# A fused attention and feed-forward layer on one core: nine fills, the first tile's path, the burst form and the instruction order changed together

## The chip, the cores and the metric

The kernel runs on one core of one Trainium2 chip. A core has five engines with instruction streams of their own: TensorE (PE in the profile; its weight loads are PEld), VectorE (DVE), ScalarE (ACT), GpSimd (POOL) and SyncE (SP), which issues most DMAs. The metric is the device time in microseconds; three runs of the kernel before gave 149.11, 149.41 and 149.48, so the median is 149.41.

## The reference

```
xn = layernorm(x)                                   # x: 1 x 2048 x 448, no scale or shift
q, k, v = split(xn @ wqkv)                          # 16 heads of 28
s = softmax(q . k[t - 2j], j = 0..7) @ v[t - 2j]    # 8 taps, dilation 2, masked before the start
s = s @ wo                                          # 448 x 448
h = gelu(xn @ w1 + b1)                              # 448 x 1792
g = silu(h @ w2 + b2)                               # 1792 x 448
out = x + s * g
```

Inputs and output are bf16.

## The kernel before

The 2048 positions are taken as two halves (even and odd positions, so that dilation 2 becomes neighbours) and cut into 16 tiles of 128; four tiles make a chunk (`c` 0 to 3). The work per tile or chunk:

- `stats`, `rstds`, `norm` (lines 432 to 517): layer norm statistics on DVE, the inverse root by ACT (square root) and DVE (reciprocal) for tiles 0 to 3 and by POOL for the others, scaling on DVE, a copy of the last 64 columns (POOL or DVE, line 482), then xn transposed: by TensorE with copies out of PSUM for tiles 0 to 3, by a transposing DMA on SP's queue for the others.
- `qk_rows` and `vproj`: q, k and v from xn; `ff1` and `ff2`: the two layers of the feed-forward part; `final`: the product with `wo`, then product with g and addition of x (`gated`).
- `attn`: nine visits of 228 positions. The scores (line 809, four PSUM banks), exponentials on ACT (line 818), masks on DVE (line 824), then P V (line 843, a burst of 64 small matmuls on eight 64x32 tiles of the array), whose result DVE transposes (line 855), normalises (859, 863) and transposes back (880).

448 rows are three and a half k-tiles. So two products of the same size run as a pair on the upper and lower half of the array (`pair`): first four passes, then a nop on POOL or SP that tells the second half it may start (line 574), then three passes with the halves exchanged. The first two tiles run as full-array matmuls instead (`first_batch`), three k-tiles for each of q, k, v, and the half k-tile at the end.

The eight PSUM banks are shared by all products. Two passes of a neighbouring pair are laid inside most P V bursts (`INSIDE`); the burst's sequence is a string in which a digit stands for one P V matmul on a tile of the array and a letter for one strip of the laid-in pass. `BURSTS` gives each visit its string: EVEN for visits 0, 3 and 4, LATER for 1, 6 and 8, MIXED[0] for 2 and 5, MIXED[1] for 7.

The order is written out. The code first adds every step as a task with engine, cost, dependencies and pool slots; `ORDER` then lists task numbers (a negative number n means task -n - 1 on its second engine), and instructions are issued in that order on each engine, so each engine runs its own sub-sequence strictly in order. The costs and `rate` and `tail` numbers of the tasks serve only to choose buffers and to leave out fill matmuls whose planned start is after 8.0 us (line 339). Those fills (lines 336 to 340, nine of 512 columns, then of 128) keep TensorE running until the first real product.

DMA loads (lines 363 to 427): tile 0's x goes out on ACT's queue, tile 1's on SP's; of `w_in` k-tile 1 on ACT, the rest on SP; the bias b1 (`b1r`, transposed by TensorE at line 1043 and copied at 1045) on POOL's. `w1` comes in two halves of three DMAs each on SP (line 982).

Of the kernel before, what the change touches and what calls it, by code (L numbers as in the profile page):

```python
# [28 lines left out]
ORDER = [  # L29
# [42 lines left out]
]  # L72
LAST = 352
TWICE = (5, 6, 7, 8, 9, 10)
QUEUE = 20
HOPS = ("POOL", "POOL")
MASK_ON = ("DVE", 0.4)


def VISITS(bs):  # L80
    out = []
# [119 lines left out]
def kernel(  # L201
# [12 lines left out]
    nc = tc.nc  # L214
# [187 lines left out]
    def ktiles(ap):  # L402
        return ap.rearrange("(k p) c -> p k c", p=P)


    load_x(0, 1, "ACT", tail=1.65)
    load_x(1, 1, "SP", tail=1.2)
    t_w = []

# [725 lines left out]
```

## Time and profile before

| | |
|---|---|
| median of three runs | 149.41 us |
| the profiled execution | 148.85 us, of which the span from first to last instruction 147.1 us |
| ACT busy, largest group | 102.1 us; 56 GELU activations of 128x512, 687 ns each |
| DVE busy, largest group | 108.4 us; 18 transpositions of 128x512 f32, 700 ns each |
| PE, instructions on the chain that ended last | 92% of the span |
| granted TensorE clock | 0.999 |
| DMA | 19.49 MB, 132 GB/s over the span |

The profile comes from one execution. Lines are those of the kernel's file; the helpers' lines stand for many callers: 526 is every matmul of the dense products, 325 and 323 are copies out of PSUM by DVE and by ACT, 330 is every fill, 365 and 388 DMA issues. In the views an entry is followed, in brackets, by the idle time of its engine before it and by what released it. The time that TensorE is busy is modelled from the issue of its pipelined matmuls.

### The profile page before, as it was taken

The page shows a single profiled execution, that of the slowest core. Times are in us where ns is not written, and L with a number is a line of the kernel's source. Part 1 is how long each engine was busy: PE and PEld are TensorE (multiplying, and loading weights), DVE is VectorE, ACT ScalarE, POOL GpSimd, SP SyncE. Part 2 cuts the span into 40 slices and gives each one's busy share as a digit, 9 for nine tenths or more (in the row PEclk, how much of TensorE's full clock was granted, in tenths as well). Part 3 has the DMA queues.
Part 4 walks back from the last instruction along what each step waited for, and adds up shares of the span by engine and source line. Part 5 has one row for each costly group of instructions (what it writes and reads, how often), then busy time and mean ns, then how long its engine had stood idle before and what let it go on. Part 6 is the DMA issues. An engine that isn't in the chain of part 4 may idle for free.

```text
span 147.1 us, 5485 instructions
## 1 busy us (share of the span) xinstructions
PE 142.4 (97%) x2273; PEld 76.1 (52%) x2273; DVE 108.4 (74%) x272; ACT 102.1 (69%) x190; POOL 29.1 (20%) x83
## 2 busy tenths in 40 slices
PE   7899999999999999999999999999999999999991
PEld 2554444444445555556555655445485454555460
DVE  2878440099555769889796988977799979699963
ACT  3459688675659487876887796985997587965320
POOL 4113570105154031612301002040001000010001
PEclk9999999999999999999999999999999999999999
DMA  4999946999759998799983498303501001002212
GB/s 107 385 328 322 134 107 137 269 159 271 185 104 159 151 242 130 174 137 207 147 193 92 138 126 166 107 21 86 170 6 36 4 0 36 4 0 62 62 67 65
DMA packets 39495, 19.49 MB, mean 132 GB/s; under 512 B 26631, under 2 KB 38762, under 8 KB 39470
## 3 DMA queue, kind: packets, MB, share of 16 engines
q1 hardware_dynamic: 38206, 17.25, 56.8%
q0 software_dynamic: 688, 1.31, 3.8%
q10 hardware_dynamic: 576, 0.57, 1.1%
q8 instruction: 18, 0.29, 0.9%
q14 instruction: 7, 0.06, 0.1%
HBM read 9.42 MB, written 3.94 MB: 91 GB/s over the span
## 4 chain that ended last, share of the span: by engine, by line
PE 92%; DMA 3%; issue 1%; DVE 1%; ACT 0%; POOL 0%; ACTq 0%; DVEq 0%; POOLq 0%
PE bank L526 82%; PE bank L764 3%; DMA E<-in_B_b_dram 3%; PE bank L809 3%; PE bank L843 3%; PE bank L942 1%; DVE sg L954 1%; ACT E L818 0%; PE bank L509 0%; DVE o L961 0%; PE bank L1043 0%; POOL E L330 0%; PE bank L762 0%; PE bank L493 0%; PE bank L338 0%
## 5 line engine op out<-in xcount | busy, mean ns | idle before, releaser
L526 PE MATMUL bank<-xnT,w 64*128 64x512 bf16 (+1 forms) x428 | 46.2, 376 | 0.0
L714 ACT ACTIVATE h<-bank,b 128x512 bf16<-128x512 f32 x56 | 35.5, 687 | 13.8 <-PE bank L526 13.5
L526 PE MATMUL bank<-w,h 64*128 64x448 bf16 (+1 forms) x440 | 41.8, 349 | 0.0
L526 PE MATMUL bank<-w_in,xnT 64*128 64x448 bf16 (+2 forms) x342 | 36.3, 350 | 0.0
L526 PEld LDWEIGHTS <-w 64*128 64x128 bf16 (+1 forms) x428 | 19.3, 93 | 21.2
L526 PEld LDWEIGHTS <-h 64*128 64x128 bf16 (+1 forms) x440 | 19.6, 93 | 14.7
L526 PEld LDWEIGHTS <-xnT 64*128 64x128 bf16 (+2 forms) x342 | 16.1, 94 | 14.5 <-issue 0.4
L818 ACT ACTIVATE E<-bank 128x456 bf16<-128x456 f32 (+1 forms) x36 | 17.1, 555 | 2.7 <-PE bank L809 2.6
L323 ACT CAST qk_tok<-bank 128x448 bf16<-128x448 f32 x26 | 13.3, 537 | 5.9 <-PE bank L526 5.4
L855 DVE STREAM_TRANSPOSE wide<-bank 128x512 f32<-128x512 f32 x18 | 12.6, 700 | 3.1 <-PE bank L843 3.1
L876 POOL COPY wide<-wide 64x64 bf16<-64x64 bf16 x20 | 5.5, 279 | 43.5 <-PE bank L526 16.2
L880 DVE STREAM_TRANSPOSE oT<-wide 128x512 bf16<-128x512 bf16 x18 | 12.0, 692 | 1.5 <-POOL wide L876 1.5
L824 DVE TENSOR_TENSOR E<-E,m_gen 128x456 bf16<-128x456 bf16 (+1 forms) x32 | 11.7, 377 | 0.9 <-ACT E L818 0.9
L526 PE MATMUL bank<-wo,oT 64*128 64x448 bf16 x98 | 11.5, 349 | 0.2 <-ACT E L818 0.2
L776 DVE TENSOR_TENSOR wide<-bank,b 128x448 f32<-128x448 f32 x15 | 9.2, 619 | 3.1 <-PE bank L526 3.0
L434 DVE BATCH_NORM_STATS2 st<-x_sb 128x6 f32<-128x448 bf16 x16 | 9.7, 609 | 2.0 <-DMA x_sb<-in_A_x_dram 2.0
L863 DVE TENSOR_TENSOR wide<-wide,rd 128x448 bf16<-128x448 f32 x18 | 11.0, 614 | 0.2
L474 DVE TENSOR_SCALAR xn<-x_sb,mv,rstd 128x448 bf16<-128x448 bf16 x16 | 6.3, 397 | 5.8 <-POOL rstd L456 5.2
L325 DVE CAST v_tok<-bank 128x448 bf16<-128x448 f32 x4 | 2.5, 615 | 9.0 <-PE bank L526 9.0
L694 ACT ACTIVATE kd<-qkT,head 128x1024 bf16<-128x1024 bf16 x8 | 8.9, 1159 | 0.0
L843 PEld LDWEIGHTS <-v 64*32 64x32 bf16 x576 | 6.9, 89 | 3.6 <-issue 3.5
L788 ACT ACTIVATE wide<-wide 128x448 f32<-128x448 f32 x12 | 6.7, 578 | 2.3 <-DVE wide L776 2.3
(78 smaller groups left out, 141.3 us busy)
## 6 DMA issues: line engine op xcount, KB each, us to landing
v<-v_hbm SPq DMA_DIRECT2D x17, 128.0 KB, 3.5
v_hbm<-v_tok SPq DMA_DIRECT2D x11, 128.0 KB, 2.9
w<-in_B_w_dram SPq DMA_DIRECT2D x2, 672.0 KB, 6.3
out_dram<-o SPq DMA_DIRECT2D x9, 112.0 KB, 1.7
x_sb<-in_A_x_dram SPq DMA_DIRECT2D x4, 224.0 KB, 2.8
w<-in_B_w_dram SPq DMA_DIRECT2D x2, 448.0 KB, 6.1
w_in<-in_A_wqkv_dram SPq DMA_DIRECT2D x2, 336.0 KB, 4.2
w<-in_B_w_dram SPq DMA_DIRECT2D x2, 336.0 KB, 5.4
```

Of the source, the lines that this page charges most:

```text
L323: nc.scalar.copy(o, i)
L434: nc.vector.bn_stats(out=buf(p_st, k)[:], in_=x_sb[:, t, :])
L526: return nc.tensor.matmul(ps[rows, :n], lhsT[:, rows], rhs, start=start, stop=stop)
L694: nc.scalar.activation(dst, src, ACT.Copy, scale=head[:, a:a + 1])
L714: nc.scalar.activation(buf(p_h, own, i)[:], buf(p_b, own, i)[:], ACT.Gelu_apprx_tanh, bias=b1[:, mt:mt + 1])
L776: nc.vector.tensor_tensor(out=buf(p_y, k)[:, :n], in0=buf(p_b, own, i)[:, :n], in1=b2[:, cs], op=ALU.add)
L818: nc.scalar.activation(buf(p_E, k)[:, :8 * n], buf(p_b, a, at + i)[:, :8 * n], ACT.Exp, scale=SCALE)
L824: nc.vector.tensor_tensor(out=E, in0=E, in1=m[:, :, :, :n].rearrange("p i g q -> p (i g) q"), op=ALU.mult)
L843: nc.tensor.matmul(banks[a][32 * g:32 * g + 32, c0:c0 + n], buf(*v_at[b])[r, s, 2 * g + h, :], buf(p_E, exps[2 * h + s // 2])[r, c1:c1 + n ...
L855: nc.vector.transpose(buf(p_dt, k)[:], buf(p_b, po, a)[:])
L863: nc.vector.tensor_tensor(out=turned_in(d[a]).rearrange("p l b c -> p (l b) c")[:, :, :DH], in0=buf(p_dt, d[a])[:].rearrange("p (b c) -> p ...
L880: nc.vector.transpose(oT[:, a::2, q:q + 256], turned_in(d[a]).rearrange("p l b c -> p l (b c)"))
```

## The change

The two added steps of tile 0 (a second part of its normalisation and of its first copy) shift the later task numbers by two, so all of `ORDER` is written anew. The diff, cut to its core:

```diff
-EVEN = TILES * 3 + STRIPS + TILES * 2 + STRIPS + TILES * 3
-LATER = TILES * 3 + STRIPS + TILES * 2 + TILES[:2] + STRIPS + TILES[2:] + TILES * 2
-MIXED = ("436501724360172435067123eadcbhfg623765334147675655acbhefd6g020101742051420751432",
-         "376124057613405271634527agfhdebc014212031050311500gedhcfab6466473642573257632475")
-BURSTS = [EVEN, LATER, MIXED[0], EVEN, EVEN, MIXED[0], LATER, MIXED[1], LATER]
+BURST_OF = TILES * 3 + STRIPS + TILES * 2 + STRIPS + TILES * 3
...
-    t_qz = [plan.add("DVE", 0.08, memset("vector", q[:, :, :, DH:], 0.0), [t_on]) for q in qk_tok]
-    t_vw = [plan.add("DVE", 0.08, memset("vector", v[:, :, :, DH:], 1.0), [t_on]) for v in v_tok]
-    t_kz = plan.add("DVE", 0.12, memset("vector", qkT[:, :, :, :PAD], 0.0), [t_on])
+    t_qz = [plan.add("POOL", 0.2, memset("gpsimd", q[:, :, :, DH:], 0.0), [t_on]) for q in qk_tok]
+    t_vw = [plan.add("POOL", 0.2, memset("gpsimd", v[:, :, :, DH:], 1.0), [t_on]) for v in v_tok]
+    t_kz = plan.add("POOL", 0.2, memset("gpsimd", qkT[:, :, :, :PAD], 0.0), [t_on])
...
-    load_x(0, 1, "ACT", tail=1.65)
-    load_x(1, 1, "SP", tail=1.2)
+    load_x(0, 1, "SP", tail=1.55)
+    load_x(1, 1, "ACT", tail=1.3, issue=0.5)
...
     def norm(t):
-        def f1(k):
-            nc.vector.tensor_scalar(buf(p_xn, k)[:, :D], x_sb[:, t, :], mv[:, t, 0:1], rstd[:, t:t + 1],
-                                    op0=ALU.subtract, op1=ALU.mult)
-        a = plan.add("DVE", 0.40, f1, [t_rs[t]], take=(p_xn,))
-
-        if not t:
-            t_st[1].deps.append(a)
+        cuts = (0, 2 * P, D) if not t else (0, D)
+        scaled = []
+        for lo, hi in zip(cuts, cuts[1:]):
+            def f1(k, lo=lo, hi=hi):
+                nc.vector.tensor_scalar(buf(p_xn, scaled[0] if scaled else k)[:, lo:hi], x_sb[:, t, lo:hi], mv[:, t, 0:1],
+                                        rstd[:, t:t + 1], op0=ALU.subtract, op1=ALU.mult)
+            scaled.append(plan.add("DVE", 0.40 if not lo and hi == D else 0.09 + (hi - lo) / 1440.0, f1, [t_rs[t]] + scaled,
+                                   take=() if scaled else (p_xn,)))
+        a = scaled[0]
...
-            def f4(k, k0=n * i, b=b):
-                copy(k.on, xnT[:, k0:k0 + n, t * P:(t + 1) * P], half_bank(buf(p_b, b))[:, k0:k0 + n, :])
...
+            for k0, k1 in ((0, 1), (1, 2)) if not t and not i else ((n * i, n * i + n),):
+                def f4(k, k0=k0, k1=k1, b=b):
+                    copy(k.on, xnT[:, k0:k1, t * P:(t + 1) * P], half_bank(buf(p_b, b))[:, k0:k1, :])
...
-            for c in BURSTS[b]:
+            for c in BURST_OF:
```

Besides these, only planned costs change (DMA rate 262 to 330 and 230 to 290, the tails, `bn_aggr` 0.18 to 0.12, b1's tail 3.2 to 4.75), and `ORDER`. Its new text, read as tasks, orders the places that matter here so:

- TensorE at the start: before, 20 fills ahead of tile 0's first two transpositions; now 11, then tile 1's first two transpositions, two fills, tile 0's first two, a fill, tile 1's other two, the first matmuls of tile 1 (q and v on k-tile 0), tile 0's other transpositions, and then matmuls of both tiles in turn. b1's transposition comes behind nine of these matmuls; before it came ahead of the first. Behind it, tile 3's transpositions now stand ahead of the pair qk(2), which they followed before.
- DVE at the start: the zero fill of `zero` (line 1018), eps, half, statistics and aggregate of tile 1, the same of tile 0, reciprocal and `norm` of tile 1, reciprocal of tile 0, `norm` of tile 0 in two parts (columns 0 to 255, 256 to 447), the copy of its k-tile 0, statistics and aggregate of tile 2, the copy of its k-tile 1. Before: eight fills, eps and half among them, statistics and aggregate of tile 0, statistics of tile 1, reciprocal and `norm` of tile 0, aggregate of tile 1, copy of tile 0's first two k-tiles.
- ACT: square roots of tile 1, then 0, then the copies of tile 1's two halves out of PSUM.
- POOL: the fill and DMA of b1, four of the nine fills with the identity between them, the copies of tiles 1 and 0 (line 482), a fill, tile 2's copy, a fill, tile 3's copy; two `v_tok` fills stand ahead of the nops of v(2) and ff1(0, 0), the fill of `qkT` ahead of that of ff1(0, 6). The two mask tiles (line 1032) and `head` (line 359) come later than before.
- SP: as before up to the second half of `w1`; then the padding store of `v_hbm` (line 1019, earlier than before), the first transposing DMA of q and k (tile 0), and only then the last of the three pieces of `w1`.
- Pairs up to wo(0): some change places, v(4) and qk(4), ff2(0) and ff2(4), qk(9) and qk(10), qk(11) and the v pairs around it, v(12) and qk(13) to qk(15). From wo(0) on the pairs, scores and bursts stand in the old order but for swaps inside ff1 chunk 3.
- DVE between the bursts of visits 6 and 7: before, the order was sum of ff2's tile 8 with b2 (line 776), gate of tile 6 (792), product of tile 6 (956), sum of tile 9 (776), a mask, the first transposition of burst 6 (855). Now: gate of tile 6, sum of tile 8, a mask, the first transposition of burst 6, its reciprocal, product of tile 6, addition of x for tile 6, the second transposition of burst 6, gate of tile 8, masks and other steps, the sums of tiles 11 and 10, a reciprocal, the sum of tile 9.

More of the change, by code (lines that the diff above doesn't have):

```diff
@@ L393, with load_x @@
     t_x = {}
-    def load_x(t0, n, eng="SP", deps=(), tail=1.6):
+    def load_x(t0, n, eng="SP", deps=(), tail=1.6, issue=0.45):
         src = rows(x_half, t0 * P, n * P).rearrange("(t p) d -> p t d", p=P)
         d = dma(eng, x_sb[:, t0:t0 + n, :], src, 112 * n, deps,
-                rate=262.0 if t0 < 2 * TPC else 230.0, tail=tail, share=n if eng == "SP" else 0)
+                issue=issue, rate=330.0 if t0 < 2 * TPC else 290.0, tail=tail, share=n if eng == "SP" else 0)
         for t in range(t0, t0 + n):
@@ L403, in ktiles @@
         return ap.rearrange("(k p) c -> p k c", p=P)
-    load_x(0, 1, "ACT", tail=1.65)
-    load_x(1, 1, "SP", tail=1.2)
+    load_x(0, 1, "SP", tail=1.55)
+    load_x(1, 1, "ACT", tail=1.3, issue=0.5)
     t_w = []
     def load_w(kt, tail, eng="SP"):
-        t_w.append([dma(eng, w_in[:, kt, :], A_wqkv[kt * P:(kt + 1) * P, :], 336, rate=262.0, tail=tail, share=1)])
-    load_w(0, 1.8)
-    load_w(1, 1.2, "ACT")
-    load_x(2, 1, "SP", tail=1.5)
-    load_w(2, 1.55)
-    load_x(3, 1, "SP", tail=1.6)
+        t_w.append([dma(eng, w_in[:, kt, :], A_wqkv[kt * P:(kt + 1) * P, :], 336, rate=330.0, tail=tail, share=1)])
+    load_w(0, 2.2)
+    load_w(1, 1.6, "ACT")
+    load_x(2, 1, "SP", tail=2.3)
+    load_w(2, 1.75)
+    load_x(3, 1, "SP", tail=1.95)
     tails = A_wqkv[KF:D, :].rearrange("p (w d) -> p w d", d=D)
-    t_w.append([dma("SP", w_in3[:64], tails[:, 0:3:2, :], 112, issue=0.6, rate=262.0, tail=1.7),
-                dma("SP", w_in3[64:], tails[:, 1:3, :], 112, issue=0.6, rate=262.0, tail=1.7)])
+    t_w.append([dma("SP", w_in3[:64], tails[:, 0:3:2, :], 112, issue=0.6, rate=330.0, tail=2.0),
+                dma("SP", w_in3[64:], tails[:, 1:3, :], 112, issue=0.6, rate=330.0, tail=2.0)])
     t_b1z = plan.add("POOL", 0.1, memset("gpsimd", b1r, 0.0), [t_on])
     t_b1r = dma("POOL", b1r[:NMT], B_b1.rearrange("(m f) -> m f", f=P), 4, [t_b1z])
-    t_b1r.tail = 3.2
+    t_b1r.tail = 4.75
     t_root = plan.add("ACT", 0.2, lambda _: nc.scalar.activation(sd[:, NT - 1:], eps_t[:], ACT.Sqrt), [t_eps], table=("sqrt",))
@@ L434, in f1 @@
             nc.vector.bn_stats(out=buf(p_st, k)[:], in_=x_sb[:, t, :])
-        k = plan.add("DVE", 0.63, f1, t_x[t], take=(p_st,))
+        k = plan.add("DVE", 0.64, f1, t_x[t], take=(p_st,))
         def f2(_):
             nc.vector.bn_aggr(out=mv[:, t, :], in_=buf(p_st, k)[:])
-        t_st[t] = plan.add("DVE", 0.18, f2, [k], give=((p_st, k, 0),))
+        t_st[t] = plan.add("DVE", 0.12, f2, [k], give=((p_st, k, 0),))
     t_rs = {}
@@ L472, in norm @@
     def norm(t):
-        def f1(k):
-            nc.vector.tensor_scalar(buf(p_xn, k)[:, :D], x_sb[:, t, :], mv[:, t, 0:1], rstd[:, t:t + 1],
-                                    op0=ALU.subtract, op1=ALU.mult)
-        a = plan.add("DVE", 0.40, f1, [t_rs[t]], take=(p_xn,))
-        if not t:
-            t_st[1].deps.append(a)
+        cuts = (0, 2 * P, D) if not t else (0, D)
[7 more added lines that the diff above has]
+        a = scaled[0]
         def f2(k):
             (nc.gpsimd if k.on == "POOL" else nc.vector).tensor_copy(buf(p_xn, a)[:, D:], buf(p_xn, a)[:, KF:D])
-        twice = t_dup[t] = plan.add("POOL" if t < TPC else "DVE", 0.28 if t < TPC else 0.18, f2, [a])
+        twice = t_dup[t] = plan.add("POOL" if t < TPC else "DVE", 0.28 if t < TPC else 0.18, f2, scaled[-1:])
         if t >= TPC:
@@ L512, in norm @@
             halves.append(b)
-            def f4(k, k0=n * i, b=b):
-                copy(k.on, xnT[:, k0:k0 + n, t * P:(t + 1) * P], half_bank(buf(p_b, b))[:, k0:k0 + n, :])
-            t_xT[t] = plan.add(("DVE", "ACT"), (dve(n * P, 2), act(n * P)), f4, [b] + ([t_xT01[t]] if i else []), give=((p_b, b, 0),))
-            t_xT01.setdefault(t, t_xT[t])
+            for k0, k1 in ((0, 1), (1, 2)) if not t and not i else ((n * i, n * i + n),):
+                def f4(k, k0=k0, k1=k1, b=b):
+                    copy(k.on, xnT[:, k0:k1, t * P:(t + 1) * P], half_bank(buf(p_b, b))[:, k0:k1, :])
+                w = (k1 - k0) * P
+                t_xT[t] = plan.add(("DVE", "ACT"), (dve(w, 2), act(w)), f4, [b] + ([t_xT[t]] if k0 else []), give=((p_b, b, 0),) if k1 > 1 else ())
+                t_xT01.setdefault(t, []).append(t_xT[t])
     def behind(later, earlier):
@@ L614, in f1 @@
                         j.part(buf(p_b, own or k), kt, 2, kt == 0, False)
-                    f[i, q, kt] = plan.add("PE", pe(D), f1, ([t_xT01[tiles0 + i]] if kt < 2 else j.deps[:1]) + t_w[kt] + ([f[i, q, kt - 1]] if kt else []),
+                    f[i, q, kt] = plan.add("PE", pe(D), f1, (t_xT01[tiles0 + i][:1 + kt * (not i and not tiles0)] if kt < 2 else j.deps[:1]) + t_w[kt] + ([f[i, q, kt - 1]] if kt else []),
                                            take=() if kt else (p_b,))
@@ L983, in load_w1 @@
         cs = slice(i * F // 2, (i + 1) * F // 2)
-        t_w1.append([dma("SP", w1[:, 0:3, cs], ktiles(B_w1[0:KF, cs]), 672, deps, rate=262.0, tail=1.3, share=3)]
-                    + [dma("SP", w1[64 * i:64 * i + 64, 3, cs], B_w1[KF:D, cs], 112, deps, rate=262.0, tail=1.3) for i in range(2)])
+        t_w1.append([dma("SP", w1[:, 0:3, cs], ktiles(B_w1[0:KF, cs]), 672, deps, rate=330.0, tail=2.1, share=3)]
+                    + [dma("SP", w1[64 * i:64 * i + 64, 3, cs], B_w1[KF:D, cs], 112, deps, rate=330.0, tail=2.0) for i in range(2)])
     load_w1(0, [])
@@ L1056 @@
         t_w2[i // 2].append(dma("SP", w2[:, lo:hi, :], B_w2[lo * P:hi * P, :].rearrange("(m p) c -> p m c", p=P),
-                                112 * (hi - lo), first, rate=230.0, share=hi - lo))
+                                112 * (hi - lo), first, rate=290.0, share=hi - lo))
     t_b2 = dma("POOL", b2[:], B_b2.rearrange("(o d) -> o d", o=1).to_broadcast((P, D)), 112, turned)
```

84 rows, old and new, of the table ORDER are left out of this document.

## The prediction

> **What bounds the kernel now.** I read the page's totals first.
>
> ```profile
> span 147.1 us, 5485 instructions
> PE 142.4 (97%) x2273; PEld 76.1 (52%) x2273; DVE 108.4 (74%) x272; ACT 102.1 (69%) x190; POOL 29.1 (20%) x83
> ```
>
> Then busy time by stage (columns: stretch in us, its length, then busy us and instruction count of PE, PEld, DVE, ACT, POOL, then granted clock, DMA share, GB/s).
>
> ```profile
> 6.04:11.41 5.37, 5.37 (x51) 2.92 (x49) 3.92 (x14) 3.07 (x9) 0.71 (x3) 1.00 1.07 340
> 11.41:46.63 35.22, 35.22 (x358) 16.90 (x356) 18.24 (x56) 25.73 (x43) 12.30 (x33) 1.00 0.89 184
> 46.63:103.29 56.66, 56.66 (x1203) 31.25 (x1196) 47.45 (x110) 43.25 (x83) 11.44 (x28) 1.00 0.79 140
> 103.29:105.00 1.71, 1.47 (x15) 0.59 (x12) 1.62 (x4) 1.70 (x3) 0.00 (x0) 1.00 0.62 184
> 105.00:143.15 38.15, 38.15 (x627) 21.42 (x627) 32.97 (x70) 26.17 (x51) 1.95 (x9) 1.00 0.12 35
> 143.15:147.10 3.95, 0.79 (x19) 0.64 (x16) 1.40 (x4) 0.25 (x1) 0.84 (x1) 0.97 0.20 60
> ```
>
> TensorE is busy without a hole from 6.04 to 143.15, but for 1.71 - 1.47 = 0.24 us after 103.29. Busy need not mean full pace, so I check one stretch against its work further down. The start comes next, in order of time (start us, duration us, engine, line, operation, output<-input).
>
> ```profile
> 0.81 0.41 ACTq L365 DMA_DIRECT2D x_sb<-in_A_x_dram  x1
> 0.82 0.20 POOL L330 MEMSET E<- 128x128 bf16 x1 [0.29 <-POOLq L1119]
> 0.82 0.39 SPq L365 DMA_DIRECT2D x_sb<-in_A_x_dram  x1
> ...
> 0.86 4.03 PE L338 MATMUL bank<-const-bfloat16-1.0 128*128 128x512 bf16 x20 [0.86 <-PEq L1119]
> 0.90 0.11 DVE L330 MEMSET qkT<- 128x64 uint32 x1 [0.90 <-PEq L1119]
> ...
> 3.38 0.63 DVE L434 BATCH_NORM_STATS2 st<-x_sb 128x6 f32<-128x448 bf16 x1 [1.98 <-DMA x_sb<-in_A_x_dram]
> 4.04 0.18 DVE L438 BATCH_NORM_AGGREGATE mv<-st 128x2 f32<-128x6 f32 x1
> 4.14 0.60 DVE L434 BATCH_NORM_STATS2 st<-x_sb 128x6 f32<-128x448 bf16 x1
> 4.26 0.29 ACT L446 ACTIVATE sd<-mv,eps_t 128x1 f32<-128x1 f32 x1 [1.24 <-DVE mv L438]
> ...
> 4.65 0.15 DVE L449 RECIPROCAL rstd<-sd 128x1 f32<-128x1 f32 x1
> 4.83 0.40 DVE L474 TENSOR_SCALAR xn<-x_sb,mv,rstd 128x448 bf16<-128x448 bf16 x1
> ...
> 5.29 0.28 PE L509 MATMUL bank<-ident,xn 128*128 128x128 bf16 x2 [0.40 <-DVE xn L474]
> ...
> 5.61 0.29 DVE L325 COPY xnT<-bank 128x256 bf16<-128x256 bf16 x1 [0.29 <-PE bank L509]
> ...
> 6.04 0.73 PE L526 MATMUL bank<-w_in,xnT 128*128 128x448 bf16 x3
> ...
> 6.19 0.37 ACT L323 COPY xnT<-bank 128x256 bf16<-128x256 bf16 x1 [0.54 <-PE bank L509]
> ```
>
> The head is a chain of small steps on one tile: x lands (3.38), statistics, square root, reciprocal, scaling, transposition, copy, first real matmul at 6.04. The last view is the chain of waits.
>
> ```profile
> 5.81 0.23 PE bank L1043
> ...
> 6.77 0.11 PE bank L509 x2
> ...
> 7.56 1.70 PE bank L526 x9
> ...
> 54.11 0.21 PE bank L843 x24
> ...
> 55.00 5.78 PE bank L526 x60
> ...
> 90.95 0.20 PE bank L843 x24
> ...
> 91.76 9.20 PE bank L526 x86
> ...
> 100.96 0.21 PE bank L843 x20
> ...
> 101.76 1.05 PE bank L526 x10
> ...
> 126.29 0.21 PE bank L843 x24
> ...
> 127.19 9.59 PE bank L526 x100
> ```
>
> Two transpositions cost 0.11 us of TensorE (6.77). Nine 448-column matmuls take 1.70, or 0.189 each, so 512 columns take 0.216. By the order list, 74 passes of 448 columns and 98 of 512 lie between 11.41 and 46.63: 74 x 0.189 + 98 x 0.216 = 35.2 us, against a stretch of 35.22. TensorE waits for nothing there. So a change can gain only before 6.04, in the 0.24 us, in the nine P V bursts, or in the last 3.95 us; anything else can only lose. A P V burst lasts from its first L843 piece to the long piece behind it: 0.89 (visit 0) and 0.81 (visit 4) in the form EVEN, 0.80 (visit 5) in MIXED[0], 0.90 (visit 8) in LATER.
>
> **The change part by part, against the profiled execution (148.85 us, of which 147.1 are span; the runs' median of 149.41 lies 0.56 above it).**
>
> *Head.* In the new list tile 1, now loaded by ACT, goes first, with tile 0 behind it. Tile 1's x takes the queue place that tile 0's had (0.81), so I let its statistics start at 3.38 too. But tile 0's statistics and aggregate now stand on VectorE before tile 1's reciprocal: statistics 4.14, and 0.66 later (as 3.38 to 4.04) the aggregate at 4.80; the reciprocal follows 0.10 behind it (as 4.04 to 4.14), at 4.90 instead of 4.65. That is +0.25. The first copy goes to ACT: 0.37 instead of 0.29, +0.08. The first real matmul comes at 6.04 + 0.33 = 6.37. TensorE has then more behind it: before, the transpositions of tile 1 (four) came after 6.04; now these four are done, and of tile 0 the first two: against the chain of before, four fewer stand behind the start, -0.22. The transposition of b1, at 5.81 in the shade of the copy before, is now inside the stream (about 0.06, half of the 6.77 row), and one more fill matmul may be too (0.05). Net +0.33 - 0.22 + 0.11 = **+0.22**. From below, with tile 1's x 0.2 us earlier and no fill, 0; from above +0.5, because the copy of tile 0's second k-tile now stands behind tile 2's statistics (0.63) and would end only just before the matmul that reads it. Cutting tile 0's normalisation and copy in two costs VectorE some 0.15 + 0.1 us of fixed cost, hidden, since tile 1's matmuls (three at 0.19) and a transposition cover them; without that cover it would be 0.25.
>
> *Fills.* VectorE loses nine fills of 0.11 us, most of them in the 1.98 us in which it waits for x anyway: gain 0. GpSimd takes nine at about 0.20 (the row at 0.82): 1.8 us on an engine busy 20% of the span. Four stand before the first copy of xn, the rest between copies and the nops that release the second half of a row-tile pair; a nop is at most 0.2 us later, and TensorE has another product (four passes, 0.76) in between. 0; without that cover 0.2 each for the two that stand ahead of a nop.
> The Trainium skill's page "SBUF — State Buffer", section "Who interferes with whom", says that VectorE in its two-port modes and GpSimd lock each other out for a whole instruction, which speaks against this move; by it a fill beside a normalisation would add up to 0.2 us to that tile, off the path for all but the first tile.
>
> *Bursts.* Six of nine change form. With EVEN at (0.89 + 0.81)/2 = 0.85, three MIXED lose 0.05 each and three LATER gain 0.05 each: **0**. Bounds with EVEN at 0.81 or 0.89: 3 x 0.01 - 3 x 0.09 = -0.24 and 3 x 0.09 - 3 x 0.01 = +0.24.
>
> *Queues.* SP now issues the last piece of w1 behind the first transposing DMA of q and k, and the padding store moves ahead of it.
>
> ```profile
> w<-in_B_w_dram SPq DMA_DIRECT2D x4, 112.0 KB, 6.3
> ...
> 11.13 3.76 SPq L388 DMA_TRANSPOSE qkT<-qk_tok  x2
> ```
>
> One such transposition holds SP for 1.9 us, so the piece goes out near 13.0 and lands by 19.3. The pair that first reads it (ff1, chunk 0, products 6 and 7) starts 18 passes of 448 and 21 of 512 behind the point that was 11.41: 11.63 + 18 x 0.189 + 21 x 0.216 = 19.6, and reads the fourth k-tile another 3 x 0.216 = 0.65 later. Margin about 0.9: cost 0, at most +0.5.
>
> *The rest of the list.* From the wo(0) pair on, TensorE's own order is the old one but for swaps inside chunk 3 of ff1, and in the first 100 us pairs only change places: no pass is added or dropped. The 0.24 us after 103.29 stay, since scores 6, their exponentials and the wo pair keep their order; the tail's order too. 0, with -0.24 from below.
>
> **Sum:** +0.22 + 0 + 0 + 0: 149.07 for a profiled execution of 148.85, and 149.41 + 0.22 = 149.6 as a median.
>
> **The rivals.** *A hole behind visit 8's scores (slower).*
>
> ```profile
> 109.60 0.62 DVE L776 TENSOR_TENSOR wide<-bank,b 128x448 f32<-128x448 f32 x1
> ...
> 110.79 0.62 DVE L956 SCALAR_TENSOR_TENSOR sg<-bank,g 128x448 bf16<-128x448 f32 x1
> 111.33 0.61 DVE L776 TENSOR_TENSOR wide<-bank,b 128x448 f32<-128x448 f32 x1
> ...
> 112.78 0.43 PE bank L809 x32
> ```
>
> The scores at 112.78 need four of eight PSUM banks. The sum of tile 9 (111.33), which frees a bank at 111.94, stands in the new list behind the sums of tiles 11 and 10, which themselves wait for products after these scores; so its bank is lost to them. The running pair holds two; so both the product of tile 6 (110.79, now behind a 0.7 us transposition and a reciprocal, hence done near 112.4) and the banks of burst 6 decide, of which one may still be held. VectorE has about 0.4 us of margin. If it runs later than that, TensorE waits for the rest; two f32 steps and a transposition late (2 x 0.54 + 0.7 = 1.8) would cost 1.4, half of that lateness 0.5, so I price it at 0.9: 149.6 + 0.9 = 150.5. For it: VectorE is busy 32.97 of 38.15 us in that stretch. Against: the exponentials free their banks earlier.
>
> *Bursts and hole both pay (faster):* EVEN at visit 4's 0.81 everywhere (-0.24), the 0.24 us after 103.29 gone, and the head at its lower bound of 0: 149.41 - 0.48 = 148.9. For it: visits 0 and 4 differ by 0.08 in one and the same form, so the form's own price is not known better than that. Against: nothing in that wait's order changed.
>
> *TensorE slows down again (slower).* Eleven fill matmuls, not 20, now stand before the first transposition. The eleven narrow ones of the 4.03 us take about 0.055 each, so the nine wide ones took 3.43, or 0.38 each, against 0.216 for 512 columns later: it starts at half pace. After the change fills end near 4.4, and until 6.37 there are only six transpositions and a few fills; before the hole was 0.40 (5.29). If pace halves again for about 3 us, 1.5 are lost: 151.1.
> The Trainium skill's page "TensorE: Matmul & The Clock Gate", Part 1, says that the clock falls back after an idle window of about 3.4 us; by that rule the 2 us here would not do it, and no run here shows it yet.
>
> **How the numbers follow.** What a measurement of this kernel can tell from no change is about 0.3%, 0.45 us: 148.96 to 149.86. The sum's own outcome (149.6, own range 149.1 to 150.0) gets 0.45, the hole 0.26, the faster case 0.22, the slow TensorE 0.07. Over its bounds the sum's case gives 0.04 to faster, 0.33 to same, 0.08 to slower; the faster case gives 0.21 to faster and 0.01 to same; the other two are slower. That makes faster 0.25, same 0.34, slower 0.41. The range runs from 148.7 (the faster case with a head 0.2 earlier) to 150.9 (the hole at its dearer end), which leaves out the slow TensorE and the rarer ends.
>
> **What would show it.** Right: tile 1's reciprocal near 4.90, the first real matmul near 6.37, the stretch from there full, the wait after 103.3 still about 0.24, bursts of 0.80 to 0.90. Wrong: idle TensorE rows released by VectorE ahead of scores or bursts; matmuls near 0.38 us pace after 6; a wait for w1 near 20; or a head that starts before 6.04, which would mean that x landed at another time than I let it.

## The result, and the profile after

| | before | after |
|---|---|---|
| median | 149.13 us (15 runs, 148.75 to 149.48) | 150.02 us (15 runs, 149.48 to 150.49) |
| profiled execution | 148.85 us, span 147.1 | 149.49 us, span 147.5 |

The ratio is 1.0054, with a 95% interval of 1.004 to 1.0068: the change makes the kernel slower by about 0.8 us (0.89 by the two medians). Ratios leave out single executions that lie more than 1.5% above the fastest of their kernel (one each in runs 2, 8 and 12 below), while the medians of those runs count them. Both profiled executions are at the lower end of their runs; a second profile of after comes as the last experiment.

The page of after gives these totals, and the view by stage has the columns of the prediction's (stretch, length, busy us and count of PE, PEld, DVE, ACT, POOL, granted clock, DMA share, GB/s).

```profile
PE 142.0 (96%) x2263; PEld 74.2 (50%) x2263; DVE 107.7 (73%) x265; ACT 101.6 (69%) x190; POOL 31.0 (21%) x92
```

```profile
6.44:11.22 4.78, 4.78 (x42) 2.48 (x41) 3.76 (x13) 2.31 (x8) 0.93 (x5) 1.00 1.07 305
11.22:45.80 34.58, 34.58 (x351) 16.37 (x348) 17.75 (x55) 25.92 (x43) 11.79 (x30) 1.00 1.12 213
45.80:103.18 57.38, 57.38 (x1195) 31.34 (x1186) 47.16 (x109) 45.10 (x85) 12.73 (x34) 1.00 0.61 127
103.18:105.00 1.82, 1.82 (x50) 1.08 (x44) 1.78 (x5) 1.58 (x5) 0.00 (x0) 1.00 0.22 63
105.00:142.76 37.76, 37.76 (x628) 20.23 (x625) 32.92 (x70) 24.23 (x47) 2.27 (x9) 1.00 0.14 40
142.76:147.50 4.74, 0.79 (x19) 0.65 (x16) 1.39 (x4) 0.25 (x1) 0.85 (x1) 1.00 0.18 50
```

TensorE is now full in every stretch up to 142.76, also where 0.24 us were idle before (103.18 to 105.00). It ends its main work at 142.76, 0.39 us earlier than before (143.15). The last stretch is 4.74 us instead of 3.95. So a kernel whose TensorE has finished earlier ends later.

Four places differ. First the start (timeline of after; start, duration, engine, line, operation).

```profile
3.58 0.63 DVE L430 BATCH_NORM_STATS2 st<-x_sb 128x6 f32<-128x448 bf16 x1 [2.35 <-DMA x_sb<-in_A_x_dram]
...
5.07 0.13 DVE L445 RECIPROCAL rstd<-sd 128x1 f32<-128x1 f32 x1
...
5.74 0.59 DVE L473 TENSOR_SCALAR xn<-x_sb,mv,rstd 128x256 bf16<-128x256 bf16 x2
...
5.69 0.28 PE L507 MATMUL bank<-ident,xn 128*128 128x128 bf16 x2 [0.65 <-DVE xn L473]
...
6.15 0.28 PE L507 MATMUL bank<-ident,xn 128*128 128x128 bf16 x2
...
6.44 0.55 PE L526 MATMUL bank<-w_in,xnT 128*128 128x448 bf16 x2
...
6.01 0.37 ACT L319 COPY xnT<-bank 128x256 bf16<-128x256 bf16 x1 [0.53 <-PE bank L507]
```

The first real matmul is at 6.44 (before 6.04). The scores of visit 1, in the chains of waits (start, length, what) of before and of after:

```profile
51.03 0.43 PE bank L809 x32
```

```profile
51.53 0.43 PE bank L809 x32
```

They start 0.50 later.

Second, the bursts (chain of waits of after).

```profile
54.61 0.21 PE bank L843 x24
...
55.40 6.35 PE bank L526 x66
...
125.35 0.21 PE bank L843 x24
...
126.16 10.24 PE bank L526 x106
```

Visit 0 takes 0.79 (before 0.89), visit 8 takes 0.81 (before 0.90); the nine sum to 7.29 us against 7.59. The form isn't all of it: visit 1, which now has EVEN, takes 0.91 in after, 0.85 before, and 0.78 with EVEN in run 3.

Third, the wait after the scores of visit 6. This is ScalarE around it, first before, then after.

```profile
103.11 1.28 ACT L818 ACT_TABLE_LOAD   x1 [1.61 <-PE bank L809]
104.40 1.88 ACT L818 ACTIVATE E<-bank 128x456 bf16<-128x456 f32 x4
```

```profile
101.21 0.68 ACT L714 ACTIVATE h<-bank,b 128x512 bf16<-128x512 f32 x1
101.91 1.28 ACT L818 ACT_TABLE_LOAD   x1
103.43 1.88 ACT L818 ACTIVATE E<-bank 128x456 bf16<-128x456 f32 x4 [0.24 <-PE bank L809]
```

Before, ScalarE's load of the table for the exponential (1.28 us) starts only when the scores are there: the engine is idle for 1.61 us in front of it, and the exponentials, whose banks TensorE needs, begin 1.1 us late. After, the load stands right behind the last GELU, and the exponentials begin with the scores. In the chains of waits the load is the piece "issue" of before; these are the scores of visits 6 and 7 around it, before, then after:

```profile
102.81 0.48 PE bank L809 x32
...
103.33 1.08 issue
...
106.91 0.49 PE bank L809 x28
```

```profile
103.18 0.43 PE bank L809 x32
...
106.83 0.43 PE bank L809 x32
```

From scores to scores it is 4.10 us before and 3.65 after, so the wait cost 0.45 and not only the 0.24 in which TensorE counts as idle. Why the load waits for the scores in one order and not in the other no view shows. It waits in the profiles of before and of runs 2, 3, 4 and 7, and in none with the changed order; which of the moved steps freed it wasn't tried.

Fourth, the end. This is what the DMA view gives for 144.5 to 145 and for 145.5 to 146 of after (GB/s in 40 slices of 12.5 ns; then queue, packets, MB, share of 16 engines), and its row for the last store on SP's queue (number, size, us from issue to landing).

```profile
GB/s 225 56 113 169 338 113 394 282 225 338 282 282 338 394 282 282 394 169 394 394 169 282 242 441 384 113 313 400 272 57 471 215 344 144 1014 215 430 143 287 215
...
q14 instruction: 1, 0.01, 7.4%
```

```profile
GB/s 0 72 0 0 72 0 0 72 0 0 72 0 0 72 0 0 72 0 0 0 0 0 0 0 0 72 0 0 0 72 0 0 16 15 15 15 15 15 15 15
```

```profile
out_dram<-o SPq DMA_DIRECT2D x1, 112.0 KB, 2.5
```

And the same store before, with the slices of 145.5 to 146 there:

```profile
GB/s 216 287 143 143 144 144 1 144 16 77 139 108 123 138 169 231 140 139 123 123 139 93 77 47 31 31 16 15 0 0 0 0 0 0 0 0 0 0 0 0
...
out_dram<-o SPq DMA_DIRECT2D x1, 112.0 KB, 1.7
```

Queue 14 carries instructions. One packet of it, which occupies one DMA engine for 7.4% x 16 x 0.5 = 0.59 us, falls among the last stores. When the others have finished, packets of 72 GB/s in single slices (72 x 12.5 ns = 900 bytes, one row of 448 columns) still come one after the other; I read them as the rest of one engine's share, though the view doesn't name the engine. The store lands 2.5 us after its issue instead of 1.7. Before, the packet of queue 14 came at 143.5, ahead of these stores. From the end of the last VectorE step to the end of the span it is 2.4 us before (147.1 - 144.50 - 0.21) and 3.2 after (147.5 - 144.11 - 0.21).

The marks of the two profiles add up. The head costs 0.50; the bursts give back 0.30, the stretch from scores 6 to scores 7 another 0.45, and the scores of visit 7, less interrupted than before, 0.14: TensorE ends 0.39 earlier. The end costs 0.79, so the span is 0.40 longer. But the execution is 0.64 longer (149.49 against 148.85). The other 0.24 lie outside the span from first to last instruction, where no view shows anything. They aren't chance: time less span is 1.95 us at the median of the 15 executions of after, and 1.74 in the 35 of before that were taken beside runs 1 to 4.

### The profile page after: what moved, and what is told of

Its sections match the earlier page's. It is cut to its first block, busy times and chain, and to the rows that moved or that the text cites. A ratio compares the mean times of both kernels' runs of the same rounds, so it can differ in the third digit from the quotient of the medians.

```text
span 147.5 us, 5475 instructions
## 1 busy us (share of the span) xinstructions
PE 142.0 (96%) x2263; PEld 74.2 (50%) x2263; DVE 107.7 (73%) x265; ACT 101.6 (69%) x190; POOL 31.0 (21%) x92
## 4 chain that ended last, share of the span: by engine, by line
PE 93%; DVE 3%; DMA 2%; issue 0%; DVEq 0%
PE bank L526 83%; PE bank L764 3%; PE bank L809 3%; PE bank L843 2%; DMA x_sb<-in_A_x_dram 2%; PE bank L942 1%; DVE st L430 1%; DVE sg L954 1%; DVE xn L473 1%; PE bank L507 0%; DVE o L961 0%; DVE mv L434 0%; PE bank L762 0%; DVE rstd L445 0%; PE bank L491 0%
## 5 line engine op out<-in xcount | busy, mean ns | idle before, releaser
L526 PEld LDWEIGHTS <-h 64*128 64x128 bf16 (+1 forms) x440 | 18.5, 93 | 15.6
L876 POOL COPY wide<-wide 64x64 bf16<-64x64 bf16 x20 | 6.0, 309 | 51.6 <-PE bank L809 12.3
L319 ACT CAST qk_tok<-bank 128x448 bf16<-128x448 f32 x26 | 12.7, 542 | 3.8 <-PE bank L526 3.2
L473 DVE TENSOR_SCALAR xn<-x_sb,mv,rstd 128x448 bf16<-128x448 bf16 (+2 forms) x17 | 6.2, 381 | 9.4 <-POOL rstd L452 9.2
L843 PEld LDWEIGHTS <-v 64*32 64x32 bf16 x576 | 6.8, 89 | 3.6 <-issue 3.1
L319 ACT CAST v_tok<-bank 128x448 bf16<-128x448 f32 x12 | 6.1, 533 | 3.7 <-ACT kd L694 0.9
```

The source lines that it names most:

```text
L319: nc.scalar.copy(o, i)
L526: return nc.tensor.matmul(ps[rows, :n], lhsT[:, rows], rhs, start=start, stop=stop)
L843: nc.tensor.matmul(banks[a][32 * g:32 * g + 32, c0:c0 + n], buf(*v_at[b])[r, s, 2 * g + h, :], buf(p_E, exps[2 * h + s // 2])[r, c1:c1 + n ...
```

## The experiments

All times are medians; each ratio is against the kernel before, in runs on the same chip.

**1. More fills in the changed kernel.** TensorE's array starts at half pace (prediction). Is it the fills that are missing?

```diff
 ORDER (changed kernel)
- ... 10, 11, 90, 91, ...                          # 11 fills, then tile 1's statistics
+ ... 10, 11, 12, 13, 14, 15, 16, 17, 90, 91, ...
```

> The changed kernel with six narrow fills more ahead of its first transposition (17 instead of 11). Theory A, the array's half pace: in the changed kernel's profile the nine wide fills all ran at 0.43 us, in the profile of before the eighth and ninth at about 0.22; if the array is still at half pace at the first real matmuls in most runs, more fills shorten this, and the time falls by 0.3 to 0.5 us, to 149.5 to 149.7. Theory B, the order of steps on VectorE and the landing of x set the head: the first transposition waits for the normalised tile at 5.69 with or without fills, and the time stays at 150.0 within 0.15. With either, the first transposition stays near 5.7 in the profile.

149.94, ratio 1.0048 (1.0031 to 1.0065), and the first transposition at 5.70: theory B. Fills neither cause the loss nor cure it.

**2. Fewer fills in the kernel before.**

```diff
 ORDER (before): fills 12 to 20 taken from ahead of tile 0's transposition and put last (not issued)
```

> The kernel before with nine fewer fills ahead of its first transposition (11 instead of 20), nothing else moved. Theory A: half pace lasts longer, the time rises by 0.3 to 0.5 us, to 149.4 to 149.6, and the profile shows first products at 0.38 us pace or a later start than 6.04. Theory B: the first transposition waits for the normalised tile anyway; 149.1 within 0.15, first real matmul 6.04 within 0.1.

149.37, ratio 1.0008 (0.9994 to 1.0022): theory B again. The first real matmul is at 6.29 and not within 0.1 of 6.04; x landed 0.14 later than in the profile of before (statistics at 3.52), and b1's transposition, ahead of that matmul, waited for its DMA until 6.05.

**3. One form of burst alone.**

```diff
-BURSTS = [EVEN, LATER, MIXED[0], EVEN, EVEN, MIXED[0], LATER, MIXED[1], LATER]
+BURSTS = [EVEN] * 9
```

> The kernel before with the form EVEN in all nine visits, nothing else. In the two profiles the nine bursts sum to 7.59 us before and 7.29 after. If the form makes this difference: visits 1 and 8 fall from 0.85 and 0.90 to about 0.80, and the time falls by 0.2 to 0.3 us, to 148.8 to 148.9. Rival, the length comes from the place and the pass laid in rather than from the string: bursts stay within 0.02 of what they were, and the time stays at 149.1 within 0.15.

148.73, ratio 0.9969 (0.9955 to 0.9983), -0.46 us. Visit 8 in its chain of waits:

```profile
126.25 0.21 PE bank L843 x23
...
126.95 0.11 PE bank L843 x21
```

It is over at 127.06, after 0.81 us. By the same reading (first L843 piece to the end of the last) visits 1, 6 and 8, which had LATER, fall by 0.06, 0.06 and 0.10, those with MIXED by 0.03 together. The profile shows -0.27 in all, just inside the interval of the runs. (Runs 9 and 10 differ in the form alone too: there the medians give -0.38 and the profiles -0.18, 7.30 against 7.48. So the form is worth 0.2 to 0.45, and the profiles show less of it than the runs.)

**4. The nine fills alone, on GpSimd.**

```diff
-    t_qz = [plan.add("DVE", 0.08, memset("vector", q[:, :, :, DH:], 0.0), [t_on]) for q in qk_tok]
+    t_qz = [plan.add("POOL", 0.2, memset("gpsimd", q[:, :, :, DH:], 0.0), [t_on]) for q in qk_tok]
 (v_tok and qkT likewise; in ORDER three ahead of the first copy of xn, three between the copies, three behind them)
```

> The kernel before with the nine fills on GpSimd, four before the first copy of xn and five between the later copies, VectorE's order else unchanged. As predicted: 0, so 149.1 within 0.15, with tile 0's copy on GpSimd still near 5.29. Rival, the fills hold up VectorE or the copies of xn's last 64 columns: the half k-tile of the first tiles comes later, +0.2 us for each that stands in front of one, at most 149.9.

149.05, ratio 1.0006 (0.9985 to 1.0027): no cost as such. The packet of queue 14 comes at 145.9 here, when the stores are through, and the last one lands after 1.7 us.

**5 to 7. Does VectorE's number of instructions place the late fetch?** Three kernels shift it without touching the work. (The counts in these expectations are rows of a listing that takes repeats together. By the pages VectorE has 272 instructions before and 265 after, 272 in run 5, 274 in run 6, 267 in run 7, 270 in run 11.)

```diff
 run 5 (changed kernel)
-    t_eps = plan.add("DVE", 0.07, memset("vector", half_t[:], -0.5), [t_eps])
+    t_eps = plan.add("DVE", 0.07, lambda _: [memset("vector", half_t[:], -0.5)(_) for i in range(8)], [t_eps])
 run 6 (changed kernel): all nine fills "POOL" -> "DVE", in ORDER right behind half_t
 run 7 (before): the four fills of qk_tok and one of v_tok "DVE" -> "POOL"
```

> The changed kernel with seven more tiny fills of the same 128x4 tile on VectorE at the start, in the 2 us in which it waits for x; nothing else differs. Theory C: an 8 KB fetch of instructions on queue 14, which occurs at 143.5 in the profile of before and at 144.9 in that of after, falls among the last stores and holds one DMA engine for 0.6 us, so the last 112 KB store lands 2.5 us after its issue instead of 1.7; where the fetch falls depends on how many instructions VectorE has behind it. With seven more it comes 1 us or more earlier: last store 1.7 us, from the last VectorE step to the end of the span 2.4 us instead of 3.2, time 149.2 to 149.4. Rival, the late landing comes from the order of the stores or from where the data lie: tail 3.2 and 150.0 as in the changed kernel.

> The changed kernel with the nine fills back on VectorE, in the 2 us in which it waits for x (that part of the change undone). Theory C: nine instructions more move the fetch on queue 14 to 143 or earlier, tail 2.4, time 149.2 to 149.4. Rival, the fills have no part in it: 150.0 within 0.15 and a tail of 3.2.

> The kernel before with five of the nine fills on GpSimd, so that VectorE has 267 instructions, as many as in the changed kernel (nine moved: 263, none moved: 272). Theory C: the fetch on queue 14 falls near 145, among the last stores, tail 3.2 us, time 149.8 within 0.2. Rival: as with all nine moved, 149.1 within 0.15 and tail 2.4.

Run 5: 149.44, ratio 1.0041 (1.0012 to 1.007); run 6: 149.52, 1.0032 (1.0007 to 1.0056); run 7: 150.46, 1.009 (1.0069 to 1.011). Five fills fewer on VectorE make the kernel before 1.15 us slower, where nine fewer cost nothing. Seven tiny instructions of no use make the changed kernel 0.6 us faster at the median, but not surely: the intervals of runs 5 and 6 overlap that of the changed kernel (1.004 to 1.0068). (In the profile of run 7 some 0.47 of that is at the start, by the scores of visit 1 at 51.63 against 51.16 in run 3; the last section comes to it.) The rows of the last store on SP's queue, runs 5 and 7:

```profile
out_dram<-o SPq DMA_DIRECT2D x1, 112.0 KB, 1.7
```

```profile
out_dram<-o SPq DMA_DIRECT2D x1, 112.0 KB, 2.9
```

In the profiles that is theory C in both directions: from the last VectorE step to the end it takes 2.4 us in run 5 and 2.5 in run 6, as before, and 3.3 in run 7. The profiled executions of runs 5 and 6 (149.01 and 148.82) are the fastest of theirs, though, so they don't stand for the rest; in the times it is run 7 that bears the theory out, and run 11 below. Runs 5 and 6 also met a second stall that I hadn't expected (chain of waits of run 5):

```profile
142.77 0.02 DVEq L954
142.79 0.40 issue
143.19 0.64 DVE sg L954
```

VectorE stands for 0.40 us at an instruction whose inputs are there (in the changed kernel it is 0.04); run 6 shows 0.31 a few steps on, run 7 shows 0.40. Their runs also spread widely, to 150.99 in run 5 and 150.84 in run 6.

**8. VectorE's order at the head.**

```diff
 ORDER (changed kernel; 86/87 statistics and aggregate of tile 0, 90/91 of tile 1, 93 and 137 reciprocal and norm of tile 1)
- 90, 91, 64, 68, 72, 86, 87, 70, 92, 93, 137, 88, 89, 129, 130
+ 64, 68, 72, 70, 90, 91, 86, 92, 93, 137, 87, 88, 89, 129, 130
```

> The changed kernel with VectorE's order at the head as before: reciprocal and norm of the first tile (tile 1) directly behind the other tile's statistics, that tile's aggregate after them. The price that I gave this step was 0.25 us. If the first transposition sets the start: reciprocal 0.15 to 0.25 earlier (at 4.85 with x landing at 3.58), first real matmul as much earlier, later marks (scores of visit 1 at 51.53) 0.2 earlier, time 149.8. Rival, tile 0, whose norm then ends 0.4 later, becomes the wait: marks the same or later, time 150.0 to 150.3. The tail stays at 3.2 with either.

150.54, ratio 1.0107 (1.0071 to 1.0142), scores of visit 1 at 51.68: the rival. The timeline of this run:

```profile
4.68 0.15 DVE L445 RECIPROCAL rstd<-sd 128x1 f32<-128x1 f32 x1
...
5.71 0.16 DVE L445 RECIPROCAL rstd<-sd 128x1 f32<-128x1 f32 x1 [0.36 <-ACT sd L442]
```

```profile
5.32 0.29 PE L507 MATMUL bank<-ident,xn 128*128 128x128 bf16 x2 [0.76 <-DVE xn L473]
...
6.31 0.29 PE L507 MATMUL bank<-ident,xn 128*128 128x128 bf16 x2 [0.59 <-DVE xn L473]
...
6.60 0.54 PE L526 MATMUL bank<-w_in,xnT 128*128 128x448 bf16 x2
```

Tile 1 is transposed 0.37 earlier than in the changed kernel (x landed 0.17 earlier), but in TensorE's order tile 0's first transposition stands ahead of the first real matmul, and it now comes at 6.31 instead of 6.15. So in the changed kernel both tiles are on the path at the start, and the order of statistics to which I gave a price of 0.25 is the better one for it. (Part of the 150.54 is the end: the last store lands after 2.9 us.)

**9 and 10. The table load alone, and with the bursts.**

```diff
                 nc.scalar.activation(buf(p_h, own, i)[:], buf(p_b, own, i)[:], ACT.Gelu_apprx_tanh,
-                                     bias=b1[:, mt:mt + 1])
+                                     bias=b1[:, mt:mt + 1]); (c, mt) == (2, 12) and nc.scalar.activation(sd[:, :1], eps_t[:], ACT.Exp)
 run 10: and BURSTS = [EVEN] * 9
```

> The kernel before with one exponential of 128x1 on ScalarE directly behind the last GELU of chunk 2. Theory D: the wait after 103.29 comes from ScalarE's table load of 1.28 us, which before starts only when the scores of visit 6 are done (103.11, 1.61 us idle in front of it) and in the changed kernel stands right behind the last GELU (101.91). With the small exponential the load runs in that idle time: exponentials start near 103.4, TensorE goes on without a hole, scores of visit 6 to scores of visit 7 take 3.65 us instead of 4.10, the time falls by 0.4 to 148.7 to 148.9. Rival, the banks or VectorE hold TensorE there all the same, or the gain is taken back by a later wait: 149.2 within 0.15.

> As the run before, and the form EVEN in all nine visits. If the two gains add (0.46 for the bursts by the runs, 0.4 for the table load): 148.3 within 0.2, faster than both kernels. Rival, one hides the other: 148.7 as with EVEN alone.

Run 9: 148.69, ratio 0.9965 (0.9948 to 0.9982). Run 10: 148.31, ratio 0.9941 (0.9922 to 0.9959), the fastest of all. ScalarE in run 10, and its chain of waits at that place:

```profile
101.57 1.28 ACT L715 ACT_TABLE_LOAD   x1
102.86 0.20 ACT L715 ACTIVATE sd<-eps_t 128x1 f32<-128x1 f32 x1
103.15 1.88 ACT L818 ACTIVATE E<-bank 128x456 bf16<-128x456 f32 x4
```

```profile
102.84 0.43 PE bank L809 x32
103.27 3.25 PE bank L526 x34
106.53 0.51 PE bank L809 x28
```

From scores to scores it is 3.69 us, against 4.10 before; the piece "issue" of 1.08 us is gone. So the late table load held up this place. In run 9 that stretch still took 3.95 in the profiled execution, with 0.11 of "issue", though its exponentials begin at 103.11 as in run 10, while its runs gained 0.5: its profile doesn't show the greater part of that gain, nor what else held TensorE there. I rest the size on run 10, where the two gains add (0.46 of run 3 and 0.51 of run 9 make 0.97; 0.89 measured).

**11. The changed kernel with five fills back on VectorE.**

```diff
-    t_qz = [plan.add("POOL", 0.2, memset("gpsimd", q[:, :, :, DH:], 0.0), [t_on]) for q in qk_tok]
+    t_qz = [plan.add("DVE", 0.08, memset("vector", q[:, :, :, DH:], 0.0), [t_on]) for q in qk_tok]
 (and qkT; in ORDER right behind half_t)
```

> The changed kernel with five of the nine fills (four of qk_tok, that of qkT) back on VectorE in its idle time at the start, so that VectorE has 272 instructions as in the kernel before. Theory C: the fetch on queue 14 again comes a microsecond ahead of the last VectorE step, as in the profiles of all kernels with 272; no late store (tail 2.4) and no stall of VectorE in the last steps (0.4 with 274 and 276): span 146.7 to 146.9, time 148.7 to 149.0, faster than before by what bursts and table load gain less the head. Rival, the changed kernel has another loss that its profile doesn't show: 149.4 or more, as with seven or nine more.

149.09, ratio 1.0001 (0.9979 to 1.0023), 0.93 less than the changed kernel (0.8 by the ratios, whose intervals don't touch), yet above the 148.7 to 149.0 expected. VectorE's last steps run without a stall, but the packet of queue 14 comes at 144.2, only just ahead of the stores, and they land after 2.1 us: the end takes 2.8 us, between 2.4 and 3.2.

Not all of the 0.93 is the end. Time less span is 1.73 us at the median here and 1.74 in run 6, as in the kernel before, against 1.95 in the changed kernel and 1.94 in run 5. Run 5 has VectorE's instructions back but the nine fills still on GpSimd, so these 0.2 us are another loss than the late fetch, and one that goes when five of the fills or more go back. Its cause is open: in run 4 the nine fills are on GpSimd too, and it is 1.75.

**12. The changed kernel once more.**

> The changed kernel once more, unchanged, for a second profile. Its first profile (149.49) is at the lower end of its runs (median 150.02); what the other 0.5 us are isn't seen in it. Theory C (the fetch on queue 14 falls among the last stores, more or less deep from run to run): the profile again shows the fetch behind the last VectorE step and a last store that lands 2.5 us or more after its issue; if the execution is a typical one, the tail is 3.4 to 3.8 us and the marks up to the last TensorE step are as in the first profile within 0.15. Rival, the rest is a wait in the middle or at the head that varies: the marks before 143 come 0.3 us or more later, tail 3.2 or less.

150.5 (8 runs, 149.44 to 151.87), ratio 1.0088 (1.0054 to 1.0122). The profiled execution is at 150.08, close to the median of the first 15 runs, though in the lower half of these 8. The marks are those of the first profile (scores of visit 1 at 51.52, last VectorE step at 144.15 against 144.11), but the last store lands later still:

```profile
q14 instruction: 1, 0.01, 1.2%
...
out_dram<-o SPq DMA_DIRECT2D x1, 112.0 KB, 2.8
```

The packet lasts 1.2% x 16 x 3.5 = 0.67 us here, and the end takes 3.4 us. Of the 0.59 us that this execution has beyond the first profile, some 0.26 are in the end (3.44 against 3.18), as expected, and 0.29 outside the span (2.28 against 1.99; the median here is 1.94). So the expectation holds by half.

Over all profiles, sorted by where the fetch falls against the start of the last VectorE step:

| kernel | VectorE instructions | fetch | last SP store | last VectorE step to the end |
|---|---|---|---|---|
| run 6 | 274 | -1.4 | 1.8 | 2.5 |
| before, runs 2, 3, 9, 10 | 272 | -1.0 | 1.7 | 2.4 |
| run 5 | 272 | -0.6 | 1.7 | 2.4 |
| run 11 | 270 | -0.1 | 2.1 | 2.8 |
| run 12 | 265 | +0.75 | 2.8 | 3.4 |
| after, run 1 | 265 | +0.8 | 2.5 | 3.2 |
| run 7 | 267 | +0.9 | 2.9 | 3.3 |
| run 8 | 265 | +1.2 | 2.9 | 3.6 |
| run 4 | 263 | +1.4 | 1.7 | 2.5 |

By and large the end grows with the lateness of the fetch, until in run 4 it comes so late that the stores are through. The fetch moves with VectorE's count, but not strictly: run 7 with 267 lies behind after with 265, and run 5 is 0.4 from the others with 272.

## Why the prediction came out as it did

The forecast was 149.6, the median is 150.02: the right side, inside the range, and 0.8 us slower than the 149.2 of before in place of 0.2. But the agreement is largely luck. The base of three runs, 149.41, stood some 0.2 us above the median of more runs and hid as much of the miss. And two gains that the sum had at nothing and a loss that it did not have at all partly cancel. Of the prediction's own signs, the wait after 103.3 was to stay, and it is gone.

- **Head, +0.22.** Right in direction, undersized, and only half right in mechanism. With x landing at the same moment (3.59 in run 3, whose head is that of before, 3.58 in after) the scores of visit 1 come at 51.16 and 51.53: +0.37. The other 0.13 of the 0.50 between the two profiles is that x landed at 3.38 in the profile of before, earlier than in the profiles of runs 2 to 4, 9 and 10 (3.52 to 3.59). The step "reciprocal at 4.90" holds within 0.02 where x lands near 3.4 (4.92 in run 12). The first real matmul is 0.28 later than in run 3 (6.44 against 6.16 in the timelines), near the +0.33 of the sum, but not by the path of the sum alone: the chain of waits of after goes through tile 0's scaling (5.74), whose cutting in two the prediction took for hidden, and its transposition (6.15). Tile 1's copy ends at 6.38, only just ahead of the matmul. The step that failed is the credit of -0.22 for four transpositions fewer behind the start. The timelines show two fewer: before, eight of 128x128 start behind 6.04 (at 6.61, 7.29 and four at 9.10), after, six behind 6.44 (6.83, 8.89, 9.78). The pair that the chain has at 6.04 started at 5.87, ahead of the matmul. And no credit is left by visit 1: from first real matmul to its scores it is 45.09 us in after and 45.00 in run 3.
- **Fills, 0.** Right for their own cost (run 4). The lockout that the prediction cites from the Trainium skill's page "SBUF — State Buffer", section "Who interferes with whom", isn't tested: in run 4 no fill runs beside a normalisation (fills at 5.65, 6.83, 8.62 and 10.66, normalisations of 0.40 at 5.02, 6.20, 7.99 and 10.03). What I hadn't seen is that moving them shifts VectorE's stream against a fetch of instructions, by the table above.
- **Bursts, 0.** Wrong: -0.46 in the runs, -0.27 in the profile. I averaged visit 0 (0.89) and visit 4 (0.81) to a price of 0.85 for EVEN. Visit 0 varies between executions: with the same form it takes 0.88 in run 3, but 0.79 in runs 2, 4, 7, 9 and 10. With 0.79 to 0.81 the lower bound that I gave (-0.24) was near the price. Why a visit takes 0.8 in one execution or order and 0.9 in another (visit 1 in after, 0.91) is not known.
- **The rest of the list, 0.** Wrong: the wait after 103.29 is gone, some -0.4 to -0.5 (0.45 between the profiles, 0.51 in run 9; from run 3 to run 10 it is 0.42). I said that scores, exponentials and wo keep their order, and they do; but I didn't ask why that wait was there. The row of the table load with its 1.61 us of idle time was in the profile of before.
- **Tail unchanged.** Wrong, and the largest term: 0.8 us in the first profile, 1.05 in that of run 12. Between the changed kernel and run 11, which differs in five fills alone, lie 0.93 us, of which 0.2 are outside the span.
- **w1's last piece.** TensorE is full from 11.22 to 45.80, so nothing waits for it; 0, as forecast.
- **The rivals.** The hole behind visit 8's scores didn't come: in after the scores stand at 112.50 with TensorE full around them. The faster case named the right two gains, at half their measured sum (0.48 against 0.89), and was undone by the end. The slow TensorE came in a small form, below.

The accounts close by the runs: run 10 is the kernel before with both gains, 148.31; run 11, the changed kernel but for five fills, has both gains too, and 149.09 (+0.78, of which its profile shows +0.45 by the scores of visit 1 and some 0.35 at the end); the changed kernel itself is at 150.02 (+0.93: 0.2 outside the span, the rest the late fetch as far as the profiles show it).

Not settled: the 0.2 us outside the span; that queue 14 fetches VectorE's own code is inferred from the table, not shown by a row that names the engine; and the stall of 0.3 to 0.4 us in runs 5 to 7 and their wide spread are seen but not explained. A version of the changed kernel's head with run 10's order behind it wasn't tried.

## What to carry to other kernels

Ask of each wait in the old profile why it is there, before you say that an edit leaves it alone: here a table load stood behind a wait of the instruction that it served. Price a form by several instances in several executions, not by the mean of two. And look at the last two microseconds for whatever moves there besides data: a handful of instructions more or fewer on one engine can put a code fetch on the last store, so a variant that changes only instruction counts is a cheap control.

## What was unexpected of the hardware

- **Code fetches share the DMA engines with the stores.** The packet of queue 14 is of some 8 KB (0.06 MB in seven packets) and lasts 0.3 to 0.7 us; in the profiles in which it meets the last stores, the end is 0.8 to 1.2 us later. That is more than the packet itself in runs 7 and 8 (0.3 and 0.4 us); why is not shown. The Trainium skill's page "Runtime: NRT & Kernel Launch", section "Instruction fetch mechanics", says that crossing a block costs one bump of a queue and is mostly hidden. At the end of this kernel it isn't hidden, by the 0.8 to 1.2 us above.
- **The array's pace at the start differs between executions.** The twenty fills that took 4.03 us in the profile of before take 5.17 in that of run 7 (nine wide ones at 0.43 and eleven narrow ones at a quarter of that make 5.0: half pace to the end):

```profile
0.86 5.17 PE L338 MATMUL bank<-const-bfloat16-1.0 128*128 128x512 bf16 x20 [0.86 <-PEq L1119]
5.82 0.42 PE L509 MATMUL bank<-ident,xn 128*128 128x128 bf16 x2
```

There the fills themselves hold up the first transposition, which has no idle time in front of it; the scores of visit 1 are 0.47 later than in run 3. In the changed kernel the first pair of transpositions takes 0.28 us in the first profile and 0.40 in run 12:

```profile
5.54 0.40 PE L507 MATMUL bank<-ident,xn 128*128 128x128 bf16 x2 [0.47 <-DVE xn L473]
```

The first real matmul comes at 6.44 in both, although x landed 0.15 earlier in run 12. The profile's granted clock reads 1.00 all the while. So the half pace can outlast 5 us of fills and then costs, by these marks, 0.15 to 0.5 us; that is what was left of the rival with the slow TensorE, and it can befall either kernel. The Trainium skill's page "TensorE: Matmul & The Clock Gate", Part 1, says that the window that decides is free-running, so that the moment of the switch varies from run to run; these profiles agree, while its figure of some 3.4 us of sustained work is passed here by more than a microsecond.
